# Loading the first batch's K, Q and v as fp32 on SyncE's queue, with the casts on VectorE, in a fused attention and SwiGLU kernel

## The chip, the cores and the metric

The kernel runs on one core of one Trainium2 chip. The metric is device time in microseconds (us), the median of several executions. Each execution also has a state, fast or slow. A profile is one execution; its span is about 1.7 us shorter than that execution's time. A ratio below is the mean time of one kernel's fast runs over the mean of the other's fast runs of the same rounds, so it is not quite the ratio of the medians that I quote.

## The reference

Eight batches of eight heads, 576 tokens, head size 64. Attention has a causal mask and a bias made from a running sum of `s`. Its output goes through an RMS norm and a SwiGLU feed-forward (FFN) of width 1536.

```python
scores = q @ k.T / sqrt(64)                         # q, k, v: (8, 8, 576, 64) fp32
cum    = cumsum(max(s, 0))                          # s: (8, 8, 576)
scores = where(causal, -1e9, scores + min(-(cum[q] - cum[k]), 0))
x      = softmax(scores) @ v                        # reshaped to 4608 tokens x 512
xn     = x / sqrt(mean(x*x) + 1e-6) * rms_g
g      = xn @ w_gate                                # 512 x 1536
out    = (silu(g) * (xn @ w_val)) @ w_out           # 1536 x 512, result (4608, 512) fp32
```

## The kernel before

The kernel first makes a list of operations, each with an estimated duration and a priority key. A greedy planner then fixes one order for each engine, and the engines work through it in order. A change to one estimate or one operation can change the order of the whole program.

Batch 0 decides when the FFN can begin. Its K and Q are loaded, transposed on TensorE, copied to `KT` and `QT`, and scored. `vwa` is v times a weight per token, made by VectorE in five row blocks. Blocks 0 and 1 are needed for the first 256 tokens, blocks 2 to 4 for the others. `xnT` is the normed, transposed attention output; the first FFN matmul reads it. On VectorE, `vwa` of blocks 2 to 4 stands **ahead** of the first `xnT` copies.

All loads of batch 0 except `s` and the norm vector are issued by GpSimd, whose loads of K, Q and the weights cast fp32 to bf16 here (a K or Q load of two heads lands as 144 KB; the fp32 load that replaces it below, as 288 KB). They form one queue: K and Q (cast by the load), v (fp32), then the weights (cast).

```python
def load_runs(b, which, h0, h1, key):               # K or Q of two heads into 64 partitions
    p0 = KP * which                                 # K in partitions 0-63, Q in 64-127
    return I("pool", "dma_start", 0.8, key=key, ...,
             out=raw[b][p0 : p0 + KP, h0:h1, :, :].rearrange("p h c d -> p h (c d)"),   # bf16
             in_=(k, q)[which][b, h0:h1, :, :].rearrange("h (p c) d -> p h (c d)", c=KC))
...
WL = (0, 2, 6, 12)                                  # weights in pieces of 256, 512, 768 columns
...
loads = [load_runs(0, w, 2 * i, 2 * i + 2, -100) for i in range(2) for w in range(2)]
...
loads += load_rows(v_nat[0], v, 0, "pool", -94)     # five loads, 256 B per (head, token)
...
loads += wl + kq1 + w2[:1] + v1 + w2[1:]
R.order(*loads)                                     # one fixed order on the queue
```

## Time and profile before

| | before |
|---|---|
| time, median of the runs beside the changed kernel | 357.61 us (356.4 to 359.5, 4 runs) |
| span of the profiled execution | 356.5 us |
| last copy of K's transposes (`KTa`) starts | 13.52 us |
| first attention half done (fourth `x_blka` ends) | 20.89 us |
| first FFN matmul (`xnT,wg_sb`) | 26.14 us |

The page's busy line of the kernel before says what bounds the whole: TensorE (PE) is busy 95% of the span. Each figure is busy us, share and number of instructions.

```profile
PE 337.4 (95%) x2946; PEld 205.6 (58%) x2946; DVE 249.8 (70%) x487; ACT 230.5 (65%) x469; POOL 132.9 (37%) x215
```

So time can only be gained where TensorE idles, and 12.6 us of its idle time lie before the first FFN matmul. The table by windows of the kernel before covers that opening: window, length, busy us (and count) of PE, PEld, DVE, ACT and POOL, TensorE's granted clock, DMA share, and GB/s as bytes written.

```profile
3.00:6.00 3.00, 0.58 (x29) 0.50 (x33) 2.01 (x4) 0.51 (x1) 2.92 (x6) 1.00 1.08 148
6.00:9.00 3.00, 1.61 (x32) 0.92 (x24) 1.67 (x5) 2.00 (x4) 2.92 (x6) 1.00 0.94 128
9.00:12.00 3.00, 2.82 (x85) 1.85 (x84) 1.69 (x4) 1.33 (x4) 3.00 (x5) 1.00 1.02 166
12.00:15.00 3.00, 2.14 (x47) 1.06 (x46) 1.74 (x3) 3.00 (x7) 2.78 (x5) 1.00 1.04 227
```

GpSimd (the fifth pair, 2.78 to 3.00 of 3.00 us) is full throughout, mostly with issuing (0.59 to 0.81 us for a K or Q load, 4.28 us for the five of v). The chain of waits of the kernel before, from 0 to 30 us (start, us, what), shows what the opening hangs on.

```profile
8.25 0.87 POOL v_nata L367
9.12 7.53 DMA v_nata<-in_v_dram
16.67 0.70 DVE vwa L367
17.41 0.43 PE psd L384 x5
...
20.47 0.43 DVE x_blka L367
```

The second row block of v is the late one: TensorE waits for `vwa`. The timeline of TensorE shows that wait in square brackets (2.27 us idle), and the start of the FFN.

```profile
17.41 0.43 PE L384 MATMUL psd<-vwa,Ea 128*128 128x65 bf16 x5 [2.27 <-DVE vwa L367]
...
26.14 1.83 PE L384 MATMUL psd<-xnT,wg_sb 128*128 128x256 bf16 x8 [0.29 <-DVE xnT L367]
```

### The profile page before, as it was taken

Reading aid. Unit: us, or ns where it says so; the run is one execution under the profiler, and the core shown is the slowest. Engines: PE = TensorE matmul, PEld = TensorE weight load, DVE = VectorE, ACT = ScalarE, POOL = GpSimd, SP = SyncE. Lnnn points to the kernel's source line nnn. Section 1 sums busy time; section 2 is a strip of 40 time slices with the busy share of each in tenths; the row PEclk is TensorE's granted clock in tenths of the full one; section 3 lists DMA queues with packets and bytes.
Section 4 is the critical chain, followed back from the end, with each engine's and each line's share of the span. In section 5 each row is a group of like instructions: output and inputs, shape, how many; then the busy total and the mean of one; then the engine's idle time right before and its main releaser. Section 6 shows DMA issues by size and latency. Waiting matters only on the chain.

```text
span 356.5 us, 7878 instructions
## 1 busy us (share of the span) xinstructions
PE 337.4 (95%) x2946; PEld 205.6 (58%) x2946; DVE 249.8 (70%) x487; ACT 230.5 (65%) x469; POOL 132.9 (37%) x215
## 2 busy tenths in 40 slices
PE   2679989999999999999999999999999999999995
PEld 1358766698669875887544454455445444444443
DVE  5486885779746995879678867887588648806840
ACT  4656999696669976767785669666798433324321
POOL 8977376140382139103920294029325100000000
PEclk9999999999999999999999999999999999999999
DMA  7999999999899998889988997979630150020002
GB/s 110 191 190 209 225 209 192 185 211 198 163 165 221 190 177 133 223 147 179 158 143 211 177 173 130 221 153 163 179 76 2 31 157 0 0 88 32 0 33 94
DMA packets 139589, 51.14 MB, mean 143 GB/s; under 512 B 127380, under 2 KB 134296, under 8 KB 139544
## 3 DMA queue, kind: packets, MB, share of 16 engines
q1 hardware_dynamic: 131832, 41.13, 57.8%
q0 software_dynamic: 7712, 9.44, 15.9%
q8 instruction: 25, 0.41, 0.5%
q14 instruction: 20, 0.16, 0.2%
HBM read 38.16 MB, written 9.44 MB: 134 GB/s over the span
## 4 chain that ended last, share of the span: by engine, by line
PE 79%; DMA 6%; DVE 5%; POOL 4%; issue 3%; ACT 1%; SPq 0%; ACTq 0%; DVEq 0%; POOLq 0%
PE psa L384 11%; PE psd L384 10%; PE psh L384 10%; PE psc L384 10%; PE psb L384 10%; PE pse L384 9%; PE psf L384 9%; PE psg L384 9%; DMA v_nata<-in_v_dram 3%; DMA k_nat<-in_k_dram 2%; POOL q_nat L367 1%; DVE Hs L367 1%; DMA QTb<-q_bf 1%; POOL ala L367 1%; DVE u_sbb L367 1%
## 5 line engine op out<-in xcount | busy, mean ns | idle before, releaser
L384 PEld LDWEIGHTS <-wg_sb 128*128 128x128 bf16 x624 | 60.4, 98 | 33.2 <-issue 1.4
L384 PEld LDWEIGHTS <-wv_sb 128*128 128x128 bf16 x624 | 59.6, 98 | 32.9 <-issue 1.9
L384 PEld LDWEIGHTS <-Hs 128*128 128x128 bf16 x444 | 41.5, 98 | 43.3 <-issue 0.3
L367 POOL TENSOR_SCALAR_AFFINE_SELECT Ea<-Ea 128x512 bf16<-128x512 bf16 x8 | 5.2, 651 | 78.9 <-ACT Ea L367 78.9
L367 DVE SCALAR_TENSOR_TENSOR x_blkb<-x_blkb,alb,gB 128x512 bf16<-128x512 bf16 x15 | 12.4, 874 | 11.5 <-POOL alb L367 11.5
L367 POOL TENSOR_TENSOR vwb<-v_nata,wT 128x512 bf16<-128x512 f32 (+1 forms) x20 | 20.4, 1048 | 0.0
L384 PE MATMUL psa<-xnT,wg_sb 128*128 128x256 bf16 (+1 forms) x116 | 19.6, 306 | 0.2 <-DVE u_sbb L367 0.2
L384 PE MATMUL psh<-xnT,wv_sb 128*128 128x256 bf16 (+1 forms) x112 | 19.6, 311 | 0.0
L367 ACT ACTIVATE sq_scr<-x_blka 128x512 bf16<-128x512 bf16 x19 | 12.0, 631 | 11.4 <-DVE x_blka L367 11.0
L384 PE MATMUL psd<-wout_sb,Hs 128*128 128x512 bf16 x72 | 17.8, 379 | 0.0
L367 ACT ACTIVATE sq_scr<-x_blkb 128x512 bf16<-128x512 bf16 x20 | 12.7, 633 | 7.8 <-DVE x_blkb L367 7.4
L384 PE MATMUL pse<-xnT,wg_sb 128*128 128x256 bf16 (+1 forms) x96 | 17.5, 317 | 0.0
L384 PE MATMUL psg<-xnT,wv_sb 128*128 128x256 bf16 (+1 forms) x100 | 16.5, 302 | 0.5 <-ACT QTb L367 0.5
L367 ACT ACTIVATE sq_scr<-q_bf 128x1024 bf16<-128x1024 bf16 (+1 forms) x18 | 16.4, 912 | 0.2
L367 ACT ACTIVATE sq_scr<-k_bf 128x1024 bf16<-128x1024 bf16 (+1 forms) x18 | 16.4, 909 | 0.0
L384 PE MATMUL psb<-wout_sb,Hs 128*128 128x512 bf16 (+1 forms) x72 | 15.9, 361 | 0.0
L384 PE MATMUL psc<-xnT,wv_sb 128*128 128x256 bf16 (+1 forms) x92 | 15.5, 305 | 0.3 <-DVE u_sbc L367 0.3
L384 PE MATMUL psd<-xnT,wg_sb 128*128 128x256 bf16 (+1 forms) x88 | 15.3, 314 | 0.3 <-DVE xnT L367 0.3
L384 PE MATMUL psc<-xnT,wg_sb 128*128 128x256 bf16 (+1 forms) x84 | 15.5, 318 | 0.0
L367 POOL TENSOR_TENSOR vwa<-v_nata,wT 128x512 bf16<-128x512 f32 (+1 forms) x15 | 15.4, 1050 | 0.0
L367 DVE CAST q_bf<-q_nat 128x512 bf16<-128x512 f32 (+1 forms) x30 | 15.1, 505 | 0.0
L384 PE MATMUL psa<-wout_sb,Hs 128*128 128x512 bf16 x60 | 14.6, 379 | 0.0
(457 smaller groups left out, 865.6 us busy)
## 6 DMA issues: line engine op xcount, KB each, us to landing
v_nata<-in_v_dram SPq DMA_DIRECT2D x24, 256.0 KB, 5.4
q_nat<-in_q_dram SPq DMA_DIRECT2D x24, 256.0 KB, 4.1
k_nat<-in_k_dram SPq DMA_DIRECT2D x24, 256.0 KB, 3.5
out_dram<-osba SPq DMA_DIRECT2D x12, 256.0 KB, 2.6
out_dram<-osbb SPq DMA_DIRECT2D x12, 256.0 KB, 2.5
out_dram<-osbc SPq DMA_DIRECT2D x11, 256.0 KB, 2.4
v_nata<-in_v_dram POOLq DMA_DIRECT2D x8, 256.0 KB, 10.4
wout_sb<-in_moe_w_out_dram POOLq DMA_DIRECT2D x2, 768.0 KB, 15.2
```

The lines of the kernel that those rows point to most:

```text
L367: o = R.add(eng, us, lambda: f(**{n: real(a) for n, a in kw.items()}), outs, ins, key=key, lat=LAT[eng], kind=kind, dma=dma, name=outs[0]. ...
L384: nc.tensor.matmul(out, lhsT=lhsT, rhs=rhs, start=st, stop=sp)
```

## The change

The intent: take K, Q and v of batch 0 off busy GpSimd. SyncE issues them without a cast, VectorE casts K and Q, and GpSimd keeps only the weights and batch 1. K and Q still land in 64 partitions each, now as fp32. The weights come in pieces of 512 and 1024 columns.

```diff
     def load_runs(b, which, h0, h1, key):
+        p = slice(KP * which, KP * which + KP)
+        if b == 0:
+            o = land[h0 // 4][p, (h0 % 4) * KC * D : (h0 % 4 + h1 - h0) * KC * D]   # fp32
+            return I("sp", "dma_start", 0.55, key=key, dma=0.42 * (h1 - h0), lags=(0.7, 1.1),
+                     out=o.rearrange("p (h x) -> p h x", h=h1 - h0), in_=i)
...
+    def run_cast(i, eng, key):                       # 128 x 1152, fp32 to bf16
+        return I(eng, "tensor_copy", 0.66, key=key, out=o, in_=x)
...
-    WL = (0, 2, 6, 12)
+    WL = (0, 4, 12)
...
+    kq0 = [load_runs(0, w, 2 * i, 2 * i + 2, -100) for i in range(HP) for w in range(2)]
-    loads += load_rows(v_nat[0], v, 0, "pool", -94)
+    v0 = load_rows(v_nat[0], v, 0, "sp", -94)
+    R.order(*kq0[0:2], sl, *kq0[2:8], g4l, *v0)      # SyncE: K, Q, s, K, Q, ..., then v
...
     for hp in range(HP):
+        last = run_cast(hp, "dve", -96)
         prep_transpose(0, hp, -80 + hp)
...
+    R.after(wl[0], last)                             # first weights after the last cast
-    loads += wl + kq1 + w2[:1] + v1 + w2[1:]
+    loads = wl + kq1 + v1 + w2
```

Cuts left out: the definitions of `i`, `o` and `x` (the casts land in a part of `xnT` that is not in use yet), names of tiles, one more column for the check of the norms, a planner limit for SyncE's queue, and one more ordering rule for the scores of batch 0.

More of the change, by code (lines that the diff above doesn't have):

```diff
@@ L199, in schedule @@
                     if o.dma and e == "sp":
-                        r = max(r, sp_free - 2.0)
+                        r = max(r, sp_free - (2.0 if o.key > 0 else 8.0))
                     can.append((o.key, o.n, r, o))
@@ L319 @@
     nrm = pers.tile([128, 2, B, 3], fp32, name="nrm")
-    rnrm = pers.tile([128, NRUN, 5], fp32, name="rnrm")
+    rnrm = pers.tile([128, NRUN, 6], fp32, name="rnrm")
     rtop = pers.tile([128, 1], fp32, name="rtop")
@@ L333, with raw @@
     q_nat = mp.tile([128, NB, DM], fp32, name="q_nat")
-    raw = [t.rearrange("p s m -> p (s m)").bitcast(bf16)[:, 0 : H * KC * D].rearrange(
-        "p (h c d) -> p h c d", h=H, c=KC) for t in (q_nat, k_nat)]
+    land = [t.rearrange("p s m -> p (s m)") for t in (k_nat, q_nat)]
+    raw1 = land[0].bitcast(bf16)
+    def raw(b, h0, h1):
+        w = KC * D
+        if b == 0:
+            o = NTOK // 2 - 4 * w * (h0 // 4)
+            return xnT[:, 2 + h0 // 4, o + h0 * w : o + h1 * w]
+        return raw1[:, h0 * w : h1 * w]
     v_nat = ring(1, [128, NB, H, D], fp32, "v_nat")
@@ L410, in load_runs @@
     def load_runs(b, which, h0, h1, key):
-        p0 = KP * which
-        return I("pool", "dma_start", 0.8, key=key, dma=(3.95, 3.35)[b] * (h1 - h0) / 8, lags=(0.9, 1.3),
-                 out=raw[b][p0 : p0 + KP, h0:h1, :, :].rearrange("p h c d -> p h (c d)"),
-                 in_=(k, q)[which][b, h0:h1, :, :].rearrange("h (p c) d -> p h (c d)", c=KC))
+        p = slice(KP * which, KP * which + KP)
+        i = (k, q)[which][b, h0:h1, :, :].rearrange("h (p c) d -> p h (c d)", c=KC)
+        if b == 0:
+            o = land[h0 // 4][p, (h0 % 4) * KC * D : (h0 % 4 + h1 - h0) * KC * D]
+            return I("sp", "dma_start", 0.55, key=key, dma=0.42 * (h1 - h0), lags=(0.7, 1.1),
+                     out=o.rearrange("p (h x) -> p h x", h=h1 - h0), in_=i)
+        return I("pool", "dma_start", 0.8, key=key, dma=3.35 * (h1 - h0) / 8, lags=(0.9, 1.3),
+                 out=raw(b, h0, h1)[p].rearrange("p (h x) -> p h x", h=h1 - h0), in_=i)
+    def run_cast(i, eng, key):
+        w = KC * D
+        o, x = raw(0, 2 * i, 2 * i + 2), land[i // 2][:, (i % 2) * 2 * w : (i % 2) * 2 * w + 2 * w]
+        if eng == "act":
+            return I("act", "activation", 0.9, key=key, out=o, in_=x, func=AF.Copy)
+        return I(eng, "tensor_copy", 0.66, key=key, out=o, in_=x)
     def load_row(dst, src, b, sc, eng, key):
@@ L437, in prep_transpose @@
         t = [lay(bank("kq", 4), bf16, "p (c t) -> p c t", n=S, c=KC) for w in range(2)]
-        mms(0.52, [(t[w][64 * j : 64 * j + 64, c, :], raw[b][KP * w : KP * w + KP, 2 * hp + j, c, :],
+        mms(0.52, [(t[w][64 * j : 64 * j + 64, c, :], raw(b, 2 * hp + j, 2 * hp + j + 1)[KP * w : KP * w + KP,
+                                                                       c * D : c * D + D],
                     ident_bf[KP * w : KP * w + KP, KP * w : KP * w + KP],
@@ L466, in raw_norm @@
     def raw_norm(b, key):
-        src = raw[b].rearrange("p h c d -> p (h c d)")
-        for i in range(5):
-            w = min(1024, H * KC * D - 1024 * i)
-            I("act", "activation", 1.17 if w > DM else 0.74, key=key, out=sq_scr[:, 0:w],
-              in_=src[:, 1024 * i : 1024 * i + w], func=AF.Square,
-              accum_out=rnrm[:, b, i : i + 1])
+        parts = [raw(b, 0, 4), raw(b, 4, 8)] if b == 0 else [raw(b, 0, 8)]
+        i = 0
+        for src in parts:
+            n = src.shape[1]
+            for c in range(0, n, 1024):
+                w = min(1024, n - c)
+                I("act", "activation", 1.17 if w > DM else 0.74, key=key, out=sq_scr[:, 0:w],
+                  in_=src[:, c : c + w], func=AF.Square, accum_out=rnrm[:, b, i : i + 1])
+                i += 1
     def prep_v(b, sc, eng, key):
@@ L648, in attention @@
         if b == 0:
-            for u in range(HP + 1, 2 * HP):
+            for u in range(HP, 2 * HP):
                 R.after(sc[u], sc[HP - 1])
@@ L708 @@
     STEP = PER / 144
-    I("sp", "dma_start", 0.5, key=-100, dma=0.5, out=s_all, in_=s.rearrange("b h s -> (b h) s"))
-    I("sp", "dma_start", 0.5, key=-90, dma=0.1, out=g4,
-      in_=moe_rms_g.rearrange("(cc p) -> cc p", p=128))
+    kq0 = [load_runs(0, w, 2 * i, 2 * i + 2, -100) for i in range(HP) for w in range(2)]
+    sl = I("sp", "dma_start", 0.5, key=-100, dma=0.5, out=s_all,
+           in_=s.rearrange("b h s -> (b h) s"))
+    g4l = I("sp", "dma_start", 0.5, key=-90, dma=0.1, out=g4,
+            in_=moe_rms_g.rearrange("(cc p) -> cc p", p=128))
     fill("dve", ones, 1.0, 0.06, key=-100)
     fill("dve", w_row[:, S : NB * 128], 0.0, 0.1, key=-100)
-    loads = [load_runs(0, w, 2 * i, 2 * i + 2, -100) for i in range(2) for w in range(2)]
     def ident(t, key):
         R.add("pool", 0.5, lambda: make_identity(nc, t), [t], [], key=key, lat=0.06).n_pool = 2
-    loads += [load_runs(0, w, 2 * i, 2 * i + 2, -98) for i in (2, 3) for w in range(2)]
     ident(ident_bf, -98.5)
     ident(ident_F, -96)
-    loads += load_rows(v_nat[0], v, 0, "pool", -94)
+    v0 = load_rows(v_nat[0], v, 0, "sp", -94)
+    R.order(*kq0[0:2], sl, *kq0[2:8], g4l, *v0)
     wl = []
@@ L734 @@
     fill("dve", nrm, 0.0, 0.08, key=-90)
+    fill("dve", rnrm, 0.0, 0.06, key=-90)
     wP = decay(-95)
     for hp in range(HP):
+        last = run_cast(hp, "dve", -96)
         prep_transpose(0, hp, -80 + hp)
@@ L749 @@
     w2 = [load_w(2, 6 * i, 6 * i + 6, -40) for i in range(2)]
-    loads += wl + kq1 + w2[:1] + v1 + w2[1:]
-    for o in loads[15:]:
+    R.after(wl[0], last)
+    loads = wl + kq1 + v1 + w2
+    for o in loads[2:]:
         R.after(o, masks[0, HP - 1])
```

## The prediction

> **What bounds the kernel now.** The page gives TensorE 337.4 us busy of 356.5 (95%), so at most 19 us are idle. The table by windows places them: 12.6 us before the first feed-forward matmul (at 26.14 us in the timeline), 1.2 us from there to 60 us, 1.2 us from 60 to 345, 4.1 us at the end. The change can pay only by starting the feed-forward earlier, without opening gaps after it.
>
> **The opening, before.** GpSimd casts while loading. It issues the eight K/Q loads from 1.32 to 7.66 us, with the bf16 identity between (ready 5.36). Their transposes start at 5.62, 9.03, 10.82 and 12.79 us. The windows show only 115 to 170 GB/s written to SBUF while K/Q land (fp32 is read at twice that), against 225 for v afterwards. v lands at 16.64: TensorE waits 2.27 us for VectorE's `vwa`. The first half of attention ends on VectorE (fourth `x_blka`) at 20.89; squares, alpha, scaling, transposes and `xnT` take another 5.25 us.
>
> **What the change does.**
> - K/Q become eight fp32 loads of 288 KB, ahead of v on SyncE. An issue costs 0.5 to 0.6 us there (`s_all` 0.59): about 5 us for eight and `s`. [...] Weights later read about 414 GB/s (207 written); at 300 to 350 GB/s read, my estimate, the last Q lands at 10.3 to 11 us, not 12.8.
> - VectorE gains four casts of 128x1152. A 128x512 cast takes 0.42 us, so I estimate 0.8 us each. All lie between load and transpose, and the instruction order puts the first two around the 1.35 us scan and ahead of the first `KTa` copy, which slips from 6.4 to about 8.4 us.
> - I expect transposes at about 5.8, 8.3, 10 and 12.1 us, the last `KTa` copy at 13 (was 13.52).
> - v's first rows land at about 13. The `vwa` wait disappears; masks and exponentials on GpSimd and ScalarE then limit the first half.
> - GpSimd loses thirteen issues of K/Q and v. Weights come in four larger loads instead of six, from about 11 us.
>
> **Sum.** The fourth `x_blka` ends at about 18.7 instead of 20.89; the first feed-forward matmul starts at about 24 instead of 26.14. Gain 2.1 us. The second weight load (1024 columns) should land at 26 to 27, the next at 31; TensorE needs them at about 28.5 and 32.5, so I charge only 0.4 us for this and the reshuffled later order.
>
> **Prediction: 355.3 us, 80% range 352.8 to 358.3.** Chances: faster by over 2% 0.03, within 2% 0.94, slower by over 2% 0.03.
>
> **What would show each step.** Right: `vwa` no longer waits for `v_nata`; last transposes of batch 0 start near 12; first `xnT,wg_sb` matmul near 24; TensorE idle before it about 2 us less, and under 2 us from there to 60. Wrong: casts waiting for `q_nat` beyond 12 us, or TensorE waiting for `wg_sb` or `wv_sb` after the start.
>
> **What would make it wrong.** fp32 rows write twice the bytes to 64 partitions: if the write side limits, K/Q land near 14 us and the start is no earlier (358). If loads run at 400 GB/s and casts cost 0.6 us, the start may come at 22.5 (353.5). Large weight loads arriving late could stall TensorE after the start and return the gain.

The forecast's sum: 2.1 us gained before the FFN, less 0.4 charged after it, 1.7 us in all, for 355.3 us.

## The result, and the profile after

The changed kernel takes **372.33 us** (372.2 to 372.41, 4 runs) against 357.61 (356.4 to 359.5, 4 runs). The ratio is 1.0406, 95% interval 1.0357 to 1.0456: 4% slower, where the prediction gave that 3 chances in 100.

TensorE has the same work and a longer span:

```profile
PE 335.7 (91%) x2917; PEld 205.7 (56%) x2946; DVE 253.1 (68%) x492; ACT 229.7 (62%) x471; POOL 120.8 (33%) x200
```

(PE counts 2917 matmuls against 2946 weight loads: 29 matmul records are missing, so small idle figures of TensorE late in the program are not to be trusted.)

The same windows of the kernel after:

```profile
3.00:6.00 3.00, 0.00 (x0) 0.00 (x0) 0.00 (x0) 0.00 (x0) 0.00 (x0) 1.00 1.03 254
6.00:9.00 3.00, 0.69 (x36) 0.56 (x36) 2.47 (x3) 0.65 (x1) 0.00 (x0) 1.00 1.01 223
9.00:12.00 3.00, 1.46 (x44) 1.26 (x45) 1.48 (x3) 1.45 (x3) 0.00 (x0) 1.00 1.05 227
12.00:15.00 3.00, 1.91 (x45) 1.05 (x43) 2.18 (x4) 2.12 (x5) 1.58 (x2) 1.00 1.22 212
```

GpSimd is free as intended. But the rate settles near 225 GB/s, not the 300 to 350 that I estimated, and K and Q are twice the bytes. The chain of waits of the kernel after, 0 to 42 us:

```profile
3.56 6.05 DMA k_nat<-in_q_dram
...
9.62 4.63 SPq L375
...
15.31 18.64 DMA v_nata<-in_v_dram
...
33.97 0.69 DVE vwa L375
...
36.93 0.70 DVE xnT L375
...
37.67 1.86 PE psb L392 x8
```

One transfer of v holds the chain for 18.64 us, from the start of its issue (2.40 us) to its landing. It is the fifth and smallest: 64 tokens, 128 KB. VectorE's timeline shows what it stopped.

```profile
16.94 1.28 DVE L375 TENSOR_TENSOR vwa<-v_nata,psg 128x512 bf16<-128x512 f32 x2
...
22.38 0.68 DVE L375 TENSOR_TENSOR vwa<-v_nata,psg 128x512 bf16<-128x512 f32 x1
28.16 0.69 DVE L375 TENSOR_TENSOR vwa<-v_nata,psg 128x512 bf16<-128x512 f32 x1 [5.10 <-DMA v_nata<-in_v_dram]
33.97 0.68 DVE L375 TENSOR_TENSOR vwa<-v_nata,psg 64x512 bf16<-64x512 f32 x1 [5.12 <-DMA v_nata<-in_v_dram]
...
36.93 0.69 DVE L375 TENSOR_TENSOR xnT<-psd,g_sb 128x512 bf16<-128x512 bf16 x1 [0.40 <-PE psd L390]
```

The first two blocks of v came in time: the wait of 2.27 us is gone, as predicted. Blocks 3 and 4 came 5 us late each, and because the `xnT` copies stand behind them in VectorE's order, those waited too (the first two start at 35.84 and 36.93 us), although they do not need these rows.

Where the time went, by landmarks in both profiles: the first FFN matmul, then the first `w_out` matmul of token chunks 1, 2, 4, 7 and 9 (of 9), read from TensorE's timeline.

| us | FFN start | chunk 1 | chunk 2 | chunk 4 | chunk 7 | chunk 9 | span |
|---|---|---|---|---|---|---|---|
| before | 26.14 | 57.79 | 92.38 | 167.32 | 279.28 | 341.88 | 356.5 |
| after | 37.67 | 69.36 | 104.19 | 181.37 | 292.72 | 355.32 | 370.5 |
| difference | +11.53 | +11.57 | +11.81 | +14.05 | +13.44 | +13.44 | +14.0 |

So 11.5 of the 14.0 us are lost before the FFN starts, and about 1.6 more between chunks 2 and 9 (13.44 less 11.81).

**Why the last rows came late.** From 13.6 us GpSimd issues the weights on its own queue. The DMA view of the kernel after for 25 to 33 us, queue by queue (packets, MB, share of 16 engines): q0 is GpSimd's, q1 is SyncE's.

```profile
q0 software_dynamic: 833, 1.67, 110.9%
q1 hardware_dynamic: 45, 0.01, 1.1%
```

In these 8 us v moved 44 rows, each a packet of 256 B (the 45th packet has 4 B), while 817 of the 833 packets of the weights had 2048 B. v was all but complete. The trace keeps start, duration and size of each packet: at 24.59 us 50 of v's 4608 rows are left, and the last starts at 33.43. Nearly all of them are 0.18 us apart. A weight packet of 2048 B takes 0.173 us (939 of 1024 such packets). So v's rest came one row for each weight packet. Fifty rows at 0.18 us make 9.0 us, and 8.84 were measured. The spacing follows the packets on the other queue: four late rows just before, beside weight packets of 1024 B (0.098 us each), are 0.105 us apart, and in e5 and e6 below late rows beside 512 B (0.060 us) are 0.067 us apart.

The records do not name the DMA engine of a packet, but they show that one share in 16 was late: each load of v also writes 16 packets of 4 B, and for the fifth load 15 of them start by 24.16 us and the last at 33.60 (for the fourth, 15 by 22.71 and the last at 27.85). After 27.85 us there are 32 rows left, a sixteenth of the fifth load's 512. Spread over 16 engines the 50 rows would have taken 0.6 us (9.0 / 16, an estimate).

Before the change v stood ahead of the weights on the same queue and was not held so long: its last packet started 2.9 us after the first weight packet (18.91 and 16.04 us), against 16.7 us after it here (33.43 and 16.72). The move also cut v's packets to a sixteenth, from 288 of 4096 B to 4608 of 256 B. No run separates the lost place from the smaller packets.

### The profile page after: what moved, and what is told of

Its sections match the earlier page's. It is cut to its first block, busy times and chain, and to the rows that moved or that the text cites. A ratio compares the mean times of both kernels' runs of the same rounds, so it can differ in the third digit from the quotient of the medians.

```text
span 370.5 us, 7858 instructions
## 1 busy us (share of the span) xinstructions
PE 335.7 (91%) x2917; PEld 205.7 (56%) x2946; DVE 253.1 (68%) x492; ACT 229.7 (62%) x471; POOL 120.8 (33%) x200
## 4 chain that ended last, share of the span: by engine, by line
PE 75%; DMA 7%; DVE 6%; POOL 4%; ACT 3%; issue 2%; SPq 2%; DVEq 0%; ACTq 0%
PE psb L392 11%; PE psg L392 10%; PE psd L392 10%; PE pse L392 9%; PE psf L392 9%; PE psh L392 9%; PE psc L392 9%; PE psa L392 8%; DMA v_nata<-in_v_dram 5%; SPq L375 2%; ACT sq_scr L375 2%; DMA k_nat<-in_q_dram 2%; DVE Hs L375 1%; POOL vwb L375 1%; POOL vwa L375 1%
## 5 line engine op out<-in xcount | busy, mean ns | idle before, releaser
L375 DVE SCALAR_TENSOR_TENSOR x_blkb<-x_blkb,alb,gB 128x512 bf16<-128x512 bf16 x15 | 11.8, 835 | 11.5 <-POOL alb L375 11.5
L392 PE MATMUL psg<-xnT,wv_sb 128*128 128x256 bf16 (+1 forms) x108 | 18.6, 308 | 0.0
L392 PE MATMUL psf<-xnT,wg_sb 128*128 128x256 bf16 (+1 forms) x99 | 17.3, 310 | 0.0
L392 PE MATMUL psd<-xnT,wv_sb 128*128 128x256 bf16 (+1 forms) x102 | 17.2, 304 | 0.0
L392 PE MATMUL psb<-xnT,wg_sb 128*128 128x256 bf16 (+1 forms) x95 | 16.3, 310 | 1.0 <-DVE xnT L375 0.9
L392 PE MATMUL psb<-wout_sb,Hs 128*128 128x512 bf16 x68 | 16.5, 379 | 0.2
L375 DVE CAST k_bf<-k_nat 128x512 bf16<-128x512 f32 (+1 forms) x30 | 15.9, 533 | 0.0
L392 PE MATMUL psh<-xnT,wv_sb 128*128 128x256 bf16 (+1 forms) x83 | 15.3, 318 | 0.2 <-DVE x_blka L375 0.2
L392 PE MATMUL psc<-wout_sb,Hs 128*128 128x512 bf16 x58 | 14.5, 379 | 0.6 <-ACT Eg L375 0.5
L392 PE MATMUL psa<-xnT,wv_sb 128*128 128x256 bf16 (+1 forms) x83 | 14.6, 310 | 0.2
L375 ACT ACTIVATE T_sba<-psb 128x512 f32<-128x512 f32 x6 | 3.6, 602 | 17.3 <-PE psb L392 17.3
```

Source lines behind the costliest of these rows:

```text
L375: o = R.add(eng, us, lambda: f(**{n: real(a) for n, a in kw.items()}), outs, ins, key=key, lat=LAT[eng], kind=kind, dma=dma, name=outs[0]. ...
L392: nc.tensor.matmul(out, lhsT=lhsT, rhs=rhs, start=st, stop=sp)
```

## The experiments

**Theory A:** moving v to another queue lost its place ahead of the weights; beside them v's rows of 256 B go one for each weight packet, as its last 50 rows did in the kernel after (0.18 us a row beside packets of 0.173 us). **Theory B:** fp32 rows into 64 partitions are limited on the write side (223 to 254 GB/s in the kernel after from 3 to 12 us), which delays K and Q and everything behind them. **Rival 1:** SyncE's queue or v's pattern is slow by itself. **Rival 2:** only the amount of queued bytes counts, not the packets. **Theory C**, for what comes after the FFN start: TensorE's clock; **its rival:** the re-planned order.

All 18 runs gave correct results. "Before" was run again on the same chip each time (medians of a set 357.5 to 358.6 us).

### First set: undo one part at a time

**e1_v_gpsimd:** v back on GpSimd's queue ahead of the weights, K and Q stay on SyncE.

```diff
-    v0 = load_rows(v_nat[0], v, 0, "sp", -94)
+    v0 = load_rows(v_nat[0], v, 0, "pool", -94)
...                                                  # v0 leaves SyncE's order
-    loads = wl + kq1 + v1 + w2
+    loads = v0 + wl + kq1 + v1 + w2
```

> The changed kernel with one part undone: v of batch 0 goes back to GpSimd's queue, in front of the weights, and stays there with a cast; K and Q stay on SyncE in fp32. Theory A [...] the last vwa of batch 0 starts before 22 us instead of 33.97, the first feed-forward matmul starts at 25 to 28 us instead of 37.7, and the time falls to 357 to 361. Rival B (the loss is the late fp32 K/Q, 14.65 us for the last pair instead of 12.8, and whatever follows from it): the start moves by less than 3 us and the time stays above 368.

(That v is cast on GpSimd's queue is a slip in this text: `v_nat` is fp32 on either queue.) Measured 367.27 us, ratio 1.026 (1.022 to 1.0299), above my range. No wait for v is left, but the FFN starts at 32.97 us. The chain of waits has a new long piece:

```profile
4.85 13.71 DMA q_nat<-in_q_dram
```

Here GpSimd issues v at 1.84 us, and now K and Q move beside it: their last cast starts at 21.39 us instead of 14.65. The contention moved from v to K and Q. Here v has the large packets again (288 of 4096 B, 0.33 us each by the median) beside K and Q's 2304 B.

**e2_hold_weights:** v stays on SyncE; the first weight load must wait until v has landed (a one-element copy from v's last rows into the weight tile makes it wait). The planner's estimate for K and Q was raised to what was measured.

```diff
+    I("pool", "tensor_copy", 0.1, key=-93.5, out=wg_sb[0:1, 0, 0:1], in_=v_nat[0][0:1, 4, 0, 0:1])
     wl = []
-    ... dma=0.42 * (h1 - h0)
+    ... dma=0.62 * (h1 - h0)
```

> The changed kernel, v still on SyncE, but a one-element GpSimd copy that reads the last rows of v and writes into wg_sb makes the first weight load wait until v has landed. (The planner's figure for a K/Q load is set to 0.62 us a head, so that it orders GpSimd's work for the measured landing.) Theory A: with nothing beside it v lands at 19 to 21 us although it stays on SyncE, the weights come 6 to 8 us later than in the changed kernel, and still the first feed-forward matmul starts earlier, at 27 to 31 us; time 359 to 365. Rival C (SyncE's queue by itself is slow for v, because of its 256-byte rows or its issue): v's last rows still land after 28 us and the time is above 372.

Measured 364.26 us, ratio 1.0176 (1.0148 to 1.0205). The last rows of v, which took 18.6 us to land in the kernel after, take 5.4 (DMA view of this run, 0 to 45 us: KB, then us to landing):

```profile
v_nata<-in_v_dram SPq DMA_DIRECT2D x1, 128.0 KB, 5.4
```

The same view of the kernel after has:

```profile
v_nata<-in_v_dram SPq DMA_DIRECT2D x1, 128.0 KB, 18.6
```

The FFN starts at 27.19 us, so 10.5 of the 11.5 us are gone. This rules out rival 1: the queue, the rows and their number are the same. The weights are now late: after the start TensorE's weight load waits 2.2 us for `wg_sb` to land, and chunk 1 is 3.0 us behind the kernel before.

**e3_128part:** each K or Q load brings two heads of one tensor into all 128 partitions. Bytes, row length and number of loads are unchanged.

```diff
+            return I("sp", "dma_start", ..., out=land[h0 // 4][:, c0 : c0 + w],
+                     in_=(k, q)[which][b, h0:h1, :, :].rearrange("h (p c) d -> (h p) (c d)", c=KC))
...                                                  # in the transposes of batch 0:
-        raw(b, 2 * hp + j, 2 * hp + j + 1)[KP * w : KP * w + KP, c * D : c * D + D]
+        raw(0, 2 * hp, 2 * hp + 2)[64 * j : 64 * j + 64, w * KC * D + c * D : w * KC * D + c * D + D]
```

> The changed kernel with the same eight K/Q loads, same bytes and same 2304-byte rows, but each load takes two heads of one tensor into all 128 partitions instead of into 64. v stays on SyncE and the weights stay as they are. If the write side of 64 partitions limits the fp32 loads (226 GB/s measured), the four casts start at about 5.2, 7, 8.6 and 10.2 us instead of 6.24, 9.7, 12.26 and 14.65, and the SBUF side moves more than 330 GB/s between 3 and 10 us. If memory or the queue limits them, nothing moves by more than 0.5 us. The whole kernel gains little by it, since v still meets the weights: 368 to 373, or even no gain at all, because the weights are issued earlier too.

Measured 360.84 us, ratio 1.0081 (1.0049 to 1.0113), far below the 368 to 373 that I expected. Set side by side, the traces of this run and of the kernel after have the same instructions in the same order on every engine, so nothing but the landing differs. The window 6 to 9 us of this run, against 223 GB/s in the kernel after:

```profile
6.00:9.00 3.00, 0.79 (x30) 0.65 (x28) 2.83 (x5) 0.83 (x2) 0.00 (x0) 1.00 1.04 385
```

Theory B holds. The DMA engines were equally busy in both (shares of 1.01 and 1.04), but a packet of 2304 B took 0.093 us here and 0.172 in the kernel after (medians, 6 to 9 us). With each load into 64 partitions the kernel after moved 223 to 254 GB/s between 3 and 12 us. There a K load fills one half of the partitions and a Q load the other; why the two together came to no more than this is not shown. With K and Q early, most of v is through before the weights start (648 rows are left when the first weight packet starts, 1795 in the kernel after), so this one edit weakens both mechanisms: the FFN starts at 24.33 us, earlier than before the change. Still the kernel is 0.8% slower than before.

**e4_128part_v_gpsimd:** both edits.

> Both: K/Q over 128 partitions on SyncE, v on GpSimd in front of the weights. Theory A with the write-side limit: last cast at about 10.5 us, all of v by 17 us, first feed-forward matmul at 22.5 to 25 us, time 352.5 to 356, which is below the kernel before. Without the write-side limit: as e1, 357 to 361.

A miss: 364.77 us, ratio 1.0198 (1.0165 to 1.023). Again K and Q suffer from v: the last cast starts at 18.37 us (11.48 in e3), the FFN at 30.45. v on the other queue is worse here than v behind K and Q on SyncE's.

### Second set: packets, the queue by itself, and the order of `s`

**e5_old_split:** the weights cut as before the change.

```diff
-    WL = (0, 4, 12)
+    WL = (0, 2, 6, 12)
```

> After with the weights cut as before the change (first pair 256 columns, then 512, then 768, instead of 512 and 1024 columns). Packet theory ([...] v 256 B, weights one written row: 512, 1024, 1536 B): about 0.65 MB of v is still out when the weights start at 14.5 us in after; beside the first pair v gets a third of 210 GB/s, beside the second a fifth. So the last row of v lands near 26 us instead of 33.9, the first FFN matmul starts near 30 us (37.7 in after), and the time is 363 to 366 us. Rival (v is late because its own issues on SyncE are slow or because its addresses are slow, whatever runs beside it): last row stays at 32 to 34 us, time 370 to 373 us.

Measured 363.97 us, ratio 1.0182 (1.015 to 1.0213). The last v load, in the DMA view of this run:

```profile
v_nata<-in_v_dram SPq DMA_DIRECT2D x1, 128.0 KB, 8.1
```

It landed at about 23.5 us, earlier than the 26 I expected, and the FFN starts at 26.86. In this run and e6, v's last 50 rows take 1.7 us rather than 8.84. The third and the fifth of the 210 GB/s were an estimate of mine from packet sizes (256 B beside 512 and 1024 B), and that was not how it went: nearly all rows move fast, and a few stragglers (7 in e5, 10 in e6) pay one weight packet each; the rows behind them come 0.014 us apart. The direction, smaller weight packets help, is as theory A says. The time came out as expected for a wrong reason: against the kernel before, another 3.6 us were lost between chunk 1 (+0.63) and chunk 9 (+4.23).

**e6_narrow:** the new plan of the FFN, but all weight loads in pieces of 256 columns (512 B rows).

```diff
-            wl.append(load_w(w, lo * 128, hi * 128, -93 + 0.1 * i))
+        for j in range(lo, hi, 2):
+            for w in range(2):
+                wl.append(load_w(w, j * 128, (j + 2) * 128, -93 + 0.1 * i))
...                                                  # the same ordering rules for the longer list
```

> After with its own FFN plan, but every weight load cut into pieces of 256 columns, so that all weight rows are 512 B as written. Packet theory: v keeps a third of about 210 GB/s to the end, 0.65 MB take 9 to 10 us, the last row of v lands near 24 us, the first FFN matmul starts near 28 us, time 361 to 365 us; more loads on GpSimd (0.8 us each) may make the last weights late by 2 to 4 us, which would show as waits for wg and wv before 60 us. Rival (only the amount of bytes queued ahead counts, not the packet size): the last row of v stays at 31 to 34 us, time 369 to 373 us.

```profile
v_nata<-in_v_dram SPq DMA_DIRECT2D x1, 128.0 KB, 7.9
```

The order of K, Q, v and weights on the queues and the bytes are those of the kernel after; only the cut of the weights differs. Nearly as many rows of v are left when the first weight packet starts (1763, against 1795). v lands 10.7 us sooner and the FFN starts at 26.16 us. Rival 2 falls. The time is 367.38 us all the same, ratio 1.0275 (1.0249 to 1.0301), outside my range: chunk 1 begins 3.2 us and chunk 2 9.1 us behind the kernel before. Eight more weight issues and a re-planned order lie in between; I did not separate them.

**e7_before_v_sync:** the kernel **before**, with v of batch 0 alone moved to SyncE.

```diff
-    loads += load_rows(v_nat[0], v, 0, "pool", -94)
+    v0 = load_rows(v_nat[0], v, 0, "sp", -94)
...                                                  # the same ordering rules for the shorter list
```

> The kernel before with one thing changed: v of batch 0 is loaded on SyncE's queue, K and Q stay bf16-casting loads on GpSimd. Theory (the cost of the change comes from two queues on the same engines, not from SyncE as such): v now goes at once, beside the K and Q casts, is complete by 8 to 14 us, and takes its bandwidth from them; the last K and Q transposes start 1 to 4 us later than 12.8 us; the weights come after K and Q on their queue, so nothing starves v. First FFN matmul between 25 and 29 us (26.1 before), time 356 to 360 us. Rival (v on SyncE is bad by itself): its last row lands after 20 us, first FFN matmul after 30 us, time over 362 us.

Measured 361.54 us, ratio 1.0098 (1.0051 to 1.0145), above my range; FFN start 27.45 us as expected. K and Q in the DMA view, 0 to 20 us, first of the kernel before and then of this run:

```profile
q_nat<-in_k_dram POOLq DMA_DIRECT2D x4, 144.0 KB, 4.7
q_nat<-in_q_dram POOLq DMA_DIRECT2D x4, 144.0 KB, 4.9
```

```profile
q_nat<-in_k_dram POOLq DMA_DIRECT2D x4, 144.0 KB, 6.8
q_nat<-in_q_dram POOLq DMA_DIRECT2D x4, 144.0 KB, 6.9
```

Splitting the queue costs K and Q 2 us each, even in the old kernel. The planner also moved work here: between the FFN start (+1.3 us against before) and chunk 9 (+3.5 us), 2.2 us more were lost.

**e9_s_later:** e3 with `s` issued two loads later.

```diff
-    R.order(*kq0[0:2], sl, *kq0[2:8], g4l, *v0)
+    R.order(*kq0[0:4], sl, *kq0[4:8], g4l, *v0)
```

> The run with 128-partition landings (360.8 us), and s issued after the second head pair's K and Q instead of after the first, since there the scan of s on VectorE ended at 7.9 us and pushed the second cast from about 6.2 to 7.97 us. If the queue order of s is what delays: casts start at about 4.6, 6.2, 7.9, 9.4 us, last copy of K transposed at about 12 us (13.6), first FFN matmul at 22.5 to 23.5 us (24.3), time 359 to 360.5 us. If TensorE's clock and the later FFN order set the time and not the prologue: the FFN starts earlier but the time stays 360 to 361.5 us, with the half-rate stretch longer.

A miss: 363.24 us, ratio 1.0157 (1.0129 to 1.0185). The casts start at 4.53, 9.03, 12.71 and 15.69 us, later instead of earlier; the core moves 266 to 297 GB/s between 8 and 14 us, where e3 had up to 392. Why the place of one load of 144 KB does this I do not know.

### Third set: repeat, clock, and the 128-partition landing in the kernel before

**e3_again:** e3 unchanged.

> The run with 128-partition landings once more, unchanged, on the chip of this set, because its sibling with s issued two loads later came out 2.4 us slower in another set with K and Q moving at 270 to 297 GB/s instead of 372 to 392. If the two loads' order is the cause, this run again shows over 370 GB/s between 6 and 10 us, its casts at 4.6, 8.0, 9.5, 11.5 us and 360 to 361.5 us. If the chip or the placement of the data is the cause, it shows under 300 GB/s there, last cast after 13 us, and 362 to 364 us.

360.98 us, ratio 1.0087 (1.0049 to 1.0124), with 350 GB/s in 6 to 9 us, a little less than I asked for: e3's result repeats, so e9's loss belongs to its order; e10 below, which keeps that order, repeats it (last cast at 15.69 us again). The FFN starts at 25.55 us here and at 24.33 in e3. One profile's opening is thus uncertain by more than a microsecond, and I read nothing from smaller differences.

**e10_s_later_warm** and **e11_warm:** e9 and e3 with eight matmuls that nobody reads, planned as operations of their own after the first mask of the second half, so that they fill TensorE's idle holes.

```diff
+    for i in range(8):
+        d = bank("warm", 1)
+        R.after(mms(0.25, [(d, ident_bf, QT[0][:, i % HP, 0:DM], True, True, False)], key=1000), masks[0, HP])
```

> The run with s after the second head pair, plus 8 matmuls of 512 columns that nothing reads, placed in TensorE's idle holes before the FFN. If order is what slowed its parent: K and Q again under 300 GB/s, casts at about 4.5, 9.0, 12.7, 15.7 us. Clock theory: the first FFN group and the second take 1.04 to 1.3 us instead of 1.87 and 1.5, worth 1 to 1.5 us; time 361.5 to 362.5 us. If the dummies do nothing for the clock: first group 1.8 to 1.9 us again, 363 us.

> The run with 128-partition landings plus the same 8 unread matmuls. Clock theory: the half-rate stretch of 24.3 to 29.5 us shrinks, the first groups take 1.04 to 1.3 us instead of 1.86, 1.90, 1.35, worth 1 to 2 us; time 1 to 2 us below the unchanged run of this set (359 to 360 if that is 360.8). Rival (the loss after the FFN start is the re-planned order, not the clock): groups get faster but the time stays within 0.5 us.

The question is the clock. In e3 the window table gives half rate (0.50) from 21 us on (the column before the last two):

```profile
21.00:24.00 3.00, 2.29 (x28) 1.97 (x28) 1.93 (x4) 0.73 (x2) 3.00 (x7) 0.50 1.11 203
24.00:27.00 3.00, 2.67 (x27) 2.14 (x27) 1.44 (x5) 0.60 (x1) 3.00 (x6) 0.50 1.12 210
```

The measured groups agree: eight FFN matmuls take 1.86 us at first and 1.04 later. In the kernel after, the table gives 0.50 to 0.51 from 24 to 41 us; TensorE waits for `vwa` three times from 21.2 us on (1.93, 5.60 and 5.54 us), and its groups take 1.86 us at 37.67 and 1.04 from 41.74 on. How long it must idle or work for the clock to change I did not measure; that added matmuls alone raise it, e18 below shows (1.83 us become 1.03). (The column does not tell all: the kernel before has 1.00 for 24 to 27 us, though its first group takes 1.83 us. There only the duration says half rate.) With the unread matmuls the first group takes 1.03 us in both runs. The times hardly moved: e11 360.79 us, ratio 1.0074 (1.0034 to 1.0113), 0.2 us below e3_again; e10 363.99, ratio 1.0161 (1.0124 to 1.0198). But the added operations also changed the planned order, so this set does not separate clock and order.

**e12_before_128:** the kernel before, all on GpSimd's queue, with K and Q landing in 128 partitions. No instruction changes place.

```diff
+        if b == 0:
+            return I("pool", ..., out=raw[0][:, h0 + which, :, :].rearrange("p c d -> p (c d)"),
+                     in_=(k, q)[which][0, h0:h1, :, :].rearrange("h (p c) d -> (h p) (c d)", c=KC))
...                                                  # transposes and norm check to match
```

> The kernel before (all loads on GpSimd's queue, K and Q cast by the load), with one thing changed: each K or Q load of two heads fills 128 partitions instead of 64, with the same rows and bytes; no instruction changes place. If the 64-partition landing held back K and Q there too: they land in 3.5 to 4.3 us instead of 4.7 to 4.9 us, the last transposes start at 11 to 12 us (12.8), first FFN matmul at 24.5 to 25.5 us (26.1), time 355.5 to 357 us against about 358. If GpSimd's issuing and casting bound them there (115 to 170 GB/s written, half of what after reached): no difference over 0.5 us anywhere.

357.41 us against 357.95, ratio 0.9988 (0.9957 to 1.0019): no difference shown. K and Q land in 4.1 and 4.3 us instead of 4.7 and 4.9. In the profile the FFN starts 2.0 us and chunk 9 begins 1.4 us earlier, which neither branch of the expectation foresaw, but the timed runs do not bear this out. So with bf16 rows and GpSimd's issuing the landing in 64 partitions costs no time that these runs show; in the change it does (e3). That the fp32 rows make the difference is likely, but no run isolates it.

### Fourth and fifth sets: clock against order

**e13_before_128_warm, e14_before_warm, e15_after_warm:** the eight unread matmuls, as in e11, in e12, in the kernel before and in the kernel after.

> The kernel before with 128-partition K and Q loads, plus the 8 unread matmuls. Its parent starts the FFN 2.0 us earlier than before (24.15 against 26.14 us) but gained only 0.1% in time, with the clock at half from 18 to 28 us. Clock theory: first groups at 1.04 us instead of 1.87 and 1.37, PV at full rate, 1 to 2 us gained: 355.5 to 357 us with before near 358. Rival (something else absorbs the earlier start): groups faster, time not more than 0.4 us from its parent's 357.4.

> The kernel before plus the 8 unread matmuls, nothing else. Only one group runs at half rate there (1.83 instead of 1.04 us), so at most 0.8 us are to be had: 357 to 358 us, ratio 0.997 to 1.000. If the unread matmuls delay the chain (6 of 0.2 to 0.6 us lie ahead of the second-half PV), the first FFN matmul comes up to 1 us later and the gain is gone.

> The kernel after plus the 8 unread matmuls. The wait for v stays (last row of v at 33 to 34.5 us, first FFN matmul 37 to 38.5 us). The holes are 5 us long there and all dummies run before the second one, so the clock may fall again: if so first groups still 1.86 and 1.24 us and time 372 to 373 us. If the clock is kept up, at most 1 us is gained: 371 to 372 us. Either way no more than 1 us of the 14.7 us is the clock; a gain of over 2 us would say that the clock was the main thing after the FFN start.

Misses, and the most useful ones. e14 takes 361.16 us, ratio 1.0079 (1.005 to 1.0108), although its FFN starts earlier (25.29 us) with every group at full rate. e13 takes 361.97, ratio 1.011 (1.0072 to 1.0147). e15's five fast runs have a median of 370.05 us (371.1 with the slow one), ratio 1.0344 (1.0296 to 1.0392). By the ratios that is 2.2 us below the kernel after, just over the 2 us that I had called a sign for the clock; but the intervals overlap; the planned order of VectorE and ScalarE changed as well, so it stays open what e15 gained, if anything.

**e16_128_pinned, e17_after128_pinned, e18_before_pinned:** seven unread matmuls inside two existing operations of e12, e3 and the kernel before. The planner's figures stay, and a comparison of the instruction lists shows the order of every engine unchanged but for the seven.

```diff
+        nwarm = {HP: 6, HP + 1: 1}.get(u, 0) if b == 0 else 0
         mms(0.19 if hf == 0 else 0.36,
+            [(full, ident_bf, QT[0][:, i % HP, 0:DM], True, True, False) for i in range(nwarm)] +
             [(AV[:, j, qb - q0, :], ...
```

> The kernel before with 128-partition K and Q loads, plus 7 unread matmuls with the order of all else kept. Clock theory: first groups 1.04 us instead of 1.87 and 1.37, the FFN start stays near 24.1 us, and the 1 to 2 us are now paid out: 355.5 to 356.7 us against about 358 of before. If the loss of the planned version (361.97 us) was the unread matmuls themselves and not the order: over 359 us again.

> The kernel after with 128-partition landings, plus the 7 unread matmuls with the order kept. Clock theory: the half-rate stretch after 24.3 us goes, worth 1.5 to 2 us: 358.8 to 359.5 us (parent 360.8 and 361.0). If it gains less than 0.5 us, the clock is not what stands between the early FFN start and the time.

> The kernel before plus the 7 unread matmuls with the order kept. One group is slow there, so 0.5 to 0.8 us are to be had: 357.2 to 357.9 us if before is 358. If the order was what made the planned version 2.6 us slower (361.16 us), this one is not slower than before; if the matmuls themselves were, it is again near 361.

| run | time, us | ratio (95%) |
|---|---|---|
| e16, e12 with them | 357.45 | 0.999 (0.9952 to 1.0029) |
| e17, e3 with them | 360.0 | 1.0053 (1.002 to 1.0086) |
| e18, before with them | 357.24 | 0.9987 (0.9953 to 1.0021) |

TensorE's timeline of e18 shows the first FFN group at full rate, 1.03 us instead of 1.83:

```profile
24.53 1.03 PE L384 MATMUL psd<-xnT,wg_sb 128*128 128x256 bf16 x8 [0.58 <-DVE xnT L367]
```

The landmarks, as differences from the kernel before in us, put clock and order apart:

| run | order | FFN start | chunk 2 | chunk 4 | chunk 7 | chunk 9 |
|---|---|---|---|---|---|---|
| e12 | kept | -1.99 | -1.59 | -1.60 | -1.39 | -1.39 |
| e18 | kept | -1.61 | -0.80 | -0.41 | -0.42 | -0.43 |
| e14 | re-planned | -0.85 | -0.18 | +2.30 | +3.44 | +3.44 |
| e3 | as after | -1.81 | -0.61 | +2.32 | +1.71 | +1.71 |
| e17 | as after | -0.53 | -0.77 | +1.47 | +0.84 | +0.85 |
| e5 | re-planned | +0.72 | +2.91 | +5.85 | +4.22 | +4.23 |
| after | re-planned | +11.53 | +11.81 | +14.05 | +13.44 | +13.44 |

e14 and e18 have nearly the same unread matmuls at the same clock; they differ in the order of everything else. By chunk 9 they are 3.9 us apart (3.44 + 0.43), in time 3.9 us by the medians of their two sets (361.16 and 357.24), or 3.3 by the ratios (0.0092 of 358). So a re-planned order (with the buffers that the planner gives out along with it) can cost over 3 us, far from the operations that caused it. In the kernels compared here the clock is worth about 1 us at most: e17 is 0.9 us below the mean of e3's two medians (with overlapping intervals), and e18 and e16 do not differ from their parents.

The traces allow one more comparison, made after the runs and forecast by none of them. Kernels whose instruction order is the same on every engine lose like amounts between chunk 2 and chunk 9, measured against the kernel before: 1.6, 2.3, 1.6 and 1.6 us in the kernel after, e3, e3_again and e17, although their FFN starts lie up to 13 us apart; 3.6 and 3.5 in e14 and e13; 0.7 and 0.5 in e1 and e4; 0.2, 0.4 and 0.9 in e12, e18 and e16, which keep the order of the kernel before.

No version beats both kernels. e12, e16 and e18 are as fast as the kernel before within their intervals. Not tried: the change in the order of the kernel before, and e2's hold on the weights together with e3's landing.

## Why the prediction was wrong, point by point

- **"TensorE ... can pay only by starting the feed-forward earlier": right.** 11.5 of 14.0 us arise before the first FFN matmul.
- **A shorter start of loads on SyncE: not seen.** Counted from the start of its issue, the first packet of K comes after 1.54 us on GpSimd in the kernel before and after 1.55 us on SyncE in the kernel after (1.04 in e3).
- **The casts: right.** I estimated 0.8 us each; they take 0.76.
- **"At 300 to 350 GB/s read, my estimate, the last Q lands at 10.3 to 11 us": wrong.** The rate was 223 to 254 GB/s and the last cast could start only at 14.65 us. The last `KTa` copy came at 16.27 us instead of the predicted 13. The cause is the landing in 64 partitions: e3 moves the same bytes into 128 at up to 385 GB/s. The prediction named this risk, but as a case in which the start is "no earlier (358)". It is a mis-sized term: the fourth `x_blka` ended at 21.31, not at 18.7, so the sum lost 2.6 us here. The sign that I had named, casts waiting for `q_nat` beyond 12 us, occurred (casts at 12.26 and 14.65 us). This lateness also helped to bring about the next step: in e3, with the same order of instructions and K and Q in time, the FFN starts at 24.33 us, close to the 24 of the prediction.
- **"v's first rows land at about 13. The `vwa` wait disappears": the step that failed, as the basis of the sum.** The wait did disappear for the two row blocks it speaks of (`vwa` at 16.94), although they landed later than forecast (the last of their 16 packets of 4 B start at 14.95 and 16.15 us). It is silent about the other three. The sum had no term for them. They measured 10.2 us of waiting on VectorE (5.10 and 5.12), and holding the weights back gave 10.5 us back (e2). With the 2.6 us above they make 12.8 of the 13.7 us by which the FFN start (37.67) missed the 24 of the prediction. What I left out was the collision of v with the weights: I thought of bandwidth for K and Q only. I did not ask what v loses by leaving the queue in which it stood ahead of the weights, nor in what packets the other queue would carry it.
- **"I charge only 0.4 us for this and the reshuffled later order": too small.** The stretch from chunk 2 to chunk 9 lost 1.6 us in the kernel after and the order alone made 3.3 us between near twins (e14 lost 3.62 between these chunks, e18 0.37). That the order causes it is shown for the pair e14 and e18. For the kernel after it is the likely cause: three other runs in its order lose 1.6 to 2.3 us there, at other starts and at another clock (e17). No run takes that order away alone.
- **"TensorE waiting for `wg_sb` or `wv_sb` after the start" as a sign of being wrong:** this did not occur. The weights came early enough; they were what made v late.
- Open: why one share in 16 of v lags, why the third v load's issue held SyncE's sequencer for 4.63 us (0.4 to 1 us for the others, 2.40 for the fifth; e2, e5 and e6 have 4.65 to 4.94 us too, so it does not explain by itself when v lands), why the place of `s` on the queue slows K and Q (e9, e10), what e6 loses by chunk 2, what e15 gained, and the last 0.6 us between +13.44 and +14.0.

## What to carry to other kernels

Before moving a load to another issuer, write down what stands behind it on its present queue: on one queue v came before the weights; on two, each of its late rows of 256 B waited for one weight packet (0.18 us a row beside 0.173 us packets). Look up in a trace what packets a queue makes of the load. Count the late rows as well as the first ones, and ask which engine's list they block (here VectorE's, 10.2 us). Where a planner orders the program, compare a change with its order pinned before believing a difference of 1%.
